# Which copy of an expert's rows the router's dot products read: PSUM or SBUF, chosen by the length of their queue

## The chip, the cores and the metric

The kernel runs on 1 core of one Trainium2 chip. The metric is device time in microseconds (us), from the first to the last instruction of one execution with what lies around it. Five engines each take their own instructions in order: TensorE (PE) multiplies matrices, VectorE (DVE) and ScalarE (ACT) work on rows, GpSimd (POOL) does element-wise work on data in SBUF and issues the gathers and scatters, SyncE (SP) issues the plain loads. They meet only in semaphores.

## The reference

Causal block attention for 4 batches and 8 heads of 576 tokens; its output is a table `x` of 2304 tokens by 512. Two mixture-of-experts layers follow, with 8 experts each and a hidden width of 1024. The second layer picks its expert from the output of the first:

```python
# layer 1, top 2 of 8 experts by noisy logits
h = np.maximum(x[mask] @ w1[e], 0.0)
out[mask] += top2_w[mask, k, None] * (h @ w2[e])
# layer 2, top 1 of 8, logits from the output of layer 1
logits = x @ w_gate + modality_bias[modality_id]
e_idx = np.argmax(logits, axis=1)
h = np.maximum(x[mask] @ w1[e], 0.0)
out[mask] = gate_w[mask, None] * (h @ w2[e])
```

## The kernel before, in words

Attention comes first, then the experts of layer 1, then those of layer 2. The experts run as a list of jobs. A job is one expert and some tiles of 128 tokens: `j00` and `j10` (the first two and three tiles of experts 0 and 1, known early), `j11` (the last two tiles of expert 1), then `firsts`: the last three tiles of expert 0, and five tiles each for experts 2 to 7. `seconds` are the groups of layer 2.

Every fp32 operand is split into a high and a low part (`wh`, `wl` for weights, `xth`, `xtl` for rows, `kp` or `hh`, `hl` for hidden values), and each product is three matmuls. For a job `run` does this:

- `mm1`: for each of 8 hidden slices f, 12 matmuls into a tile `ph` (3 buffers); ACT writes the high part of the hidden values from it, DVE the low part (SCALAR_TENSOR_TENSOR into `kp` or `hl`). `mm2` needs both.
- `mm2`: for each token tile, 24 matmuls into a tile `py` (pool `ps_y`, 3 buffers, `NY`). ACT writes `yr`, the rows of `py` scaled by their gate, to SBUF (5 buffers), POOL scatters `yr` into the table X2. In the gaps between half tiles the next job's rows are transposed (`px`, 1 buffer, filled by PE, read by ACT and DVE) into `xth`, `xtl`.
- The next weights: SP loads `raw`, ACT copies its high part `wh`, and POOL subtracts: `wl` from `raw` and `wh`, both in SBUF (`Stage.split`; in the jobs up to `firsts` always POOL, `[gps]`). Eight such pieces serve a job, four for each of its two layers.

The change touches `note`. For each finished token tile it queues eight dot products, one for each expert of layer 2, which are the logits of layer 2 piece by piece: DVE multiplies a row by a column of `wgb` (in SBUF, broadcast) and accumulates into one column of `yg`. The eighth is followed by a scatter of `yg` into the table LG on POOL. The queue is the list `fill`. `filler` takes from it between the pieces of PE's work, when the planner's clocks say that DVE is not behind. `room` is called before a `py` buffer is taken, and empties the queue until the dots that hold a `py` buffer leave one free.

A dot can read either copy of its row. `direct` says which: `py` in PSUM with the gate as the scalar, or the scaled `yr` in SBUF. Before, it is set as soon as the flag `places` is, some time after `wgb` has been asked for. So the first three tiles of all (`n` = 0, 1, 2) read `yr`, every later one `py`.

The order of PE, ACT and DVE is the order in which this code is run (a manual schedule), with estimated costs that do not depend on which copy a dot reads.

Of the kernel before, what the change touches and what calls it, by code (L numbers as in the profile page):

```python
# [30 lines left out]
def moe_kernel(tc, q, k, v, w_gate, w_noise, noise, w1, w2, mod_id, w_gate2, mod_bias, m2w1, m2w2, out):  # L31
# [72 lines left out]
    with ExitStack() as top:  # L104
# [271 lines left out]
        flags = set()  # L376
# [164 lines left out]
        fill = []  # L541
# [15 lines left out]
        places = {}  # L557
        yg_n = [0]

        def note(yr, py, g, ids, prev, then):  # L560

            n = yg_n[0]
            yg_n[0] += 1
            direct = "places" in flags

            def dot(e):
                yg = places["yg"][n % len(places["yg"])]
                vec.scalar_tensor_tensor(zero, py if direct else yr, g if direct else 1.0, wgb()[:, e], op0=OP.mult, op1=OP.mult,
                                               accum_out=yg[:, e:e + 1])
                if e == E - 1:  # L570
                    place(yg)

            def place(yg):
                i = gps.indirect_dma_start(out=LG, out_offset=bass.IndirectOffsetOnAxis(ap=ids, axis=0),
                                                 in_=yg, in_offset=None, compute_op=OP.add)
                for o in prev:
                    tc.declare_no_dep(i.ins, o.ins, reason="rows of other tokens")
                prev.append(i)
                if then:
                    then()  # L580

            t = clk["pe"] + 1
            fill.extend([(t, lambda e=e: dot(e), direct) for e in range(E)])
# [6 lines left out]
        def add_rows(ids, c0, nt, then=None):  # L590
            last = c0 + nt == NA1
            prev = last_rows if last else []
            placed_ = []

            def f(t, yr, py, g):
                c = c0 + t
                i = gps.indirect_dma_start(out=X2, out_offset=bass.IndirectOffsetOnAxis(ap=ids[:, c:c + 1], axis=0),
                                                 in_=yr, in_offset=None, compute_op=OP.add)
                for o in prev + (early_rows if last else []):
                    tc.declare_no_dep(i.ins, o.ins, reason="rows of other tokens")  # L600
                prev.append(i)
                note(yr, py, g, ids[:, c:c + 1], placed_, then if t == nt - 1 else None)
            return f
# [1069 lines left out]
```

## Time and profile before

| | |
|---|---|
| median of 3 runs | 1015.5 us (1011.27 to 1016.81) |
| the profiled execution | 1010.93 us |
| its span, first to last instruction | 1009.1 us |
| PE, DVE, ACT, POOL busy | 95%, 72%, 51%, 49% of the span |
| DVE dots reading `py` | 296 |
| DVE dots reading `yr` | 24 |

The profile is of one execution, which lies 4.6 us below the median. A time in a timeline row is the start from the beginning of the span. "idle before" in square brackets is how long the engine stood before that instruction, and what it waited for. PE is busy nearly everywhere, so the places where it stands still are few and can be looked at one by one. Jobs `j11` and the first of `firsts`, where the change lies, run from 342 to 408 us.

### The profile page before, as it was taken

What the parts mean: (1) busy time and instruction counts of PE and PEld (TensorE: products, weight loads), DVE (VectorE), ACT (ScalarE), POOL (GpSimd) and SP (SyncE); (2) the same over time, 40 slices, a digit from 0 to 9 for tenths busy, and PEclk for the clock granted to TensorE, in tenths of its full rate; (3) what the DMA queues carried; (4) which work ended last, traced back from release to release, by engine and by line L of the source; (5) the groups of instructions that cost most, each with busy time, mean ns of one, the idle gap of its engine ahead of it and who ended that gap; (6) DMA issues with size and microseconds to landing.
All of it is one profiled execution on the core that took longest, in us unless ns stands there. A gap on an engine that the chain in (4) does not pass through costs nothing.

```text
span 1009.1 us, 17454 instructions
## 1 busy us (share of the span) xinstructions
PE 959.0 (95%) x6058; PEld 866.3 (86%) x6058; DVE 728.1 (72%) x1761; ACT 518.4 (51%) x1156; POOL 496.1 (49%) x400
## 2 busy tenths in 40 slices
PE   7999998898998989999999999999999989999995
PEld 6999887787887978989989898998969879999995
DVE  6887779999967778659394866849789876445540
ACT  5999887668653244333333343333325445555551
POOL 6223333242221578968484866837377254333331
PEclk8999999999999999999999999999999999999998
DMA  5566643321065656656373645625266867666620
GB/s 125 112 165 207 192 123 84 84 70 61 27 201 169 175 115 158 158 138 126 92 144 88 148 104 129 123 73 85 82 160 181 283 215 238 224 220 224 204 89 13
DMA packets 158258, 141.59 MB, mean 140 GB/s; under 512 B 76234, under 2 KB 124746, under 8 KB 158035
## 3 DMA queue, kind: packets, MB, share of 16 engines
q1 hardware_dynamic: 140098, 107.18, 36.0%
q0 software_dynamic: 18064, 33.23, 16.4%
q8 instruction: 50, 0.82, 0.3%
q14 instruction: 46, 0.37, 0.1%
HBM read 112.54 MB, written 28.36 MB: 140 GB/s over the span
## 4 chain that ended last, share of the span: by engine, by line
PE 75%; DVE 13%; issue 4%; ACT 3%; DMA 2%; POOL 2%; SPq 1%; POOLq 0%; ACTq 0%; DVEq 0%
PE ph L71 29%; PE py L71 27%; PE pt L71 8%; PE ps L71 6%; PE pa L71 3%; PE px L71 2%; DVE wl L71 2%; DVE nm L71 2%; DVE PTl L71 2%; DMA xr<-X,ids 1%; ACT p L71 1%; DVE kp L71 1%; POOL wl L71 1%; ACT wh L71 1%; DVE sl_ob L71 1%
## 5 line engine op out<-in xcount | busy, mean ns | idle before, releaser
L71 POOL TENSOR_TENSOR wl<-raw,wh 128x1024 fp32r<-128x1024 f32 x80 | 208.3, 2633 | 107.2 <-ACT wh L71 95.3
L71 PE MATMUL ph<-xth,wh 128*128 128x320 f32 (+2 forms) x800 | 241.3, 302 | 2.1 <-DVE kp L71 2.1
L71 PE MATMUL ph<-xth,wl 128*128 128x320 f32 (+2 forms) x800 | 240.1, 300 | 0.0
L71 PE MATMUL ph<-xtl,wh 128*128 128x320 f32 (+2 forms) x800 | 240.0, 300 | 0.0
L71 DVE SCALAR_TENSOR_TENSOR zero<-py,gts,wgb 128x512 f32<-128x512 f32 x296 | 221.5, 748 | 8.2
L71 PE MATMUL py<-wh,kp 128*128 128x512 f32 x496 | 168.1, 399 | 3.9 <-DVE zero L71 3.9
L71 PEld LDWEIGHTS ph<-xth,wh 128*128 128x128 f32 x800 | 151.7, 190 | 3.7 <-DVE kp L71 2.9
L71 PEld LDWEIGHTS ph<-xtl,wh 128*128 128x128 f32 x800 | 151.7, 190 | 0.7
L71 ACT ACTIVATE wh<-raw 128x1024 fp32r<-128x1024 f32 x144 | 150.8, 1053 | 2.3 <-DMA raw<-in_moe_w_dram 2.3
L71 PEld LDWEIGHTS ph<-xth,wl 128*128 128x128 f32 x800 | 151.7, 190 | 0.0
L71 ACT ACTIVATE yr<-py,gts 128x512 f32<-128x512 f32 x60 | 41.3, 689 | 143.1 <-PE py L71 99.0
L71 PEld LDWEIGHTS py<-wh,kp 128*128 128x128 f32 x496 | 93.9, 189 | 22.7 <-DVE zero L71 4.1
L71 DVE TENSOR_TENSOR wl<-raw,wh 128x1024 fp32r<-128x1024 f32 x64 | 79.9, 1256 | 29.6 <-ACT wh L71 29.5
L71 DVE SCALAR_TENSOR_TENSOR hl<-ph,hh 128x320 fp32r<-128x320 f32 (+2 forms) x100 | 46.4, 466 | 75.2 <-ACT hh L71 74.8
L71 PE MATMUL ps<-kh,kp 128*128 128x256 f32 (+5 forms) x320 | 97.1, 346 | 3.0 <-POOL p L817 1.3
L71 PE MATMUL py<-wl,kp 128*128 128x512 f32 x248 | 97.4, 393 | 0.0
L71 POOL DMA_INDIRECT xr<-X,ids x55 | 59.0, 1073 | 75.0 <-PE px L71 45.3
L71 DVE TENSOR_TENSOR xtl<-px,xth 128x512 fp32r<-128x512 f32 x58 | 40.0, 690 | 75.6 <-ACT xth L71 75.4
L71 PE MATMUL py<-wh,hh 128*128 128x512 f32 x232 | 94.0, 405 | 0.0
L71 PE MATMUL py<-wh,hl 128*128 128x512 f32 x232 | 90.9, 392 | 0.0
L71 PE MATMUL py<-wl,hh 128*128 128x512 f32 x232 | 90.4, 390 | 0.0
L71 ACT ACTIVATE hh<-ph 128x320 fp32r<-128x320 f32 (+2 forms) x100 | 41.8, 418 | 94.3 <-PE ph L71 88.9
(249 smaller groups left out, 1841.4 us busy)
## 6 DMA issues: line engine op xcount, KB each, us to landing
raw<-in_moe_w_dram SPq DMA_DIRECT2D x144, 512.0 KB, 4.3
X<-zero SPq DMA_DIRECT2D x13, 512.0 KB, 3.6
kld<-in_k_dram SPq DMA_DIRECT2D x32, 128.0 KB, 3.1
qld<-in_q_dram SPq DMA_DIRECT2D x32, 128.0 KB, 2.9
vld<-in_v_dram SPq DMA_DIRECT2D x32, 128.0 KB, 2.6
X<-x SPq DMA_DIRECT2D x16, 256.0 KB, 2.4
xs<-in_moe_w_dram SPq DMA_DIRECT2D x4, 512.0 KB, 4.1
wgb<-WG2T POOLq DMA_DIRECT2D x1, 2048.0 KB, 8.6
```

The lines of the kernel that those rows point to most:

```text
L71: return f(*a, **kw)
```

## The change

A tile's dots read `py` only if, besides the flag, at most ten dots are queued when the tile is finished. Otherwise they read `yr`.

```diff
@@ note @@
             n = yg_n[0]
             yg_n[0] += 1
-            direct = "places" in flags
+
+            direct = "places" in flags and len(fill) <= 10
```

When tiles 3 to 6 are finished the queue is longer than ten; from tile 7 on it never is. In all 32 dots change their operand, those of the last two tiles of `j10` and of the two of `j11`.

DVE's row from the end of `mm1` of `j11` to the first `kp` of the next job, before (`zero,yg_4509<-...` is a dot, with the number of its `yg` buffer; `xtl` and `kp` are the low parts of rows and of hidden values, both read from PSUM):

```order
L71 SCALAR_TENSOR_TENSOR zero,yg_4509<-py,gts_106,wgb 128x512 x2
L71 TENSOR_TENSOR xtl<-px,xth 128x4x128
L71 SCALAR_TENSOR_TENSOR zero,yg_4509<-py,gts_106,wgb 128x512 x3
L71 TENSOR_TENSOR xtl<-px,xth 128x4x128
L71 SCALAR_TENSOR_TENSOR zero,yg_4509<-py,gts_106,wgb 128x512 x3
L71 SCALAR_TENSOR_TENSOR zero,yg_4506<-py,gts_106,wgb 128x512
L71 TENSOR_TENSOR xtl<-px,xth 128x4x128
L71 SCALAR_TENSOR_TENSOR zero,yg_4506<-py,gts_106,wgb 128x512 x5
L71 SCALAR_TENSOR_TENSOR kp_4888<-ph,kp_4888 128x384
```

These are the dots of tile 3 (`yg_4509`) and the first of tile 4 (`yg_4506`). The same place now:

```order
L71 SCALAR_TENSOR_TENSOR zero,yg_4509<-yr,wgb 128x512 x2
L71 TENSOR_TENSOR xtl<-px,xth 128x4x128
L71 SCALAR_TENSOR_TENSOR zero,yg_4509<-yr,wgb 128x512 x3
L71 TENSOR_TENSOR xtl<-px,xth 128x4x128
L71 SCALAR_TENSOR_TENSOR zero,yg_4509<-yr,wgb 128x512 x3
L71 SCALAR_TENSOR_TENSOR zero,yg_4506<-yr,wgb 128x512
L71 TENSOR_TENSOR xtl<-px,xth 128x4x128
L71 SCALAR_TENSOR_TENSOR zero,yg_4506<-yr,wgb 128x512 x5
L71 SCALAR_TENSOR_TENSOR kp_4888<-ph,kp_4888 128x384
```

Nothing moves in DVE's order: the same dots stand at the same places, between the same `xtl` and `kp`, with another operand. So it goes on to the last dot of tile 6, two dots and one `kp` or `hl` in turn.

PE's row at the start of the second tile of `j11` (tile 6), with what its instructions wait for:

```order
 L71 MATMUL px<-ident,xr 128x128 [waits DMASW4_49,DVE_49]
 L71 MATMUL px<-ident,xr 128x128 x3
-L71 MATMUL py<-wh,kp_4619 128x512 [waits DVE_49]
+L71 MATMUL py<-wh,kp_4619 128x512
 L71 MATMUL py<-wl,kp_4619 128x512
 L71 MATMUL py<-wh,kp_4619 128x512
```

The first matmul of tile 6 waited for DVE, since its `py` buffer was the one that the dots of tile 3 read. That wait is gone.

POOL's row between the second and the third weight piece for the next job:

```order
 L71 TENSOR_TENSOR wl<-raw,wh 128x1024
+L71 DMA xr<-X_60,ids_100 128x512
 L71 DMA LG<-yg_4509,ids_102 2944x9
-L71 DMA xr<-X_60,ids_100 128x512
 L71 TENSOR_TENSOR wl<-raw,wh 128x1024
```

A gather of rows and the scatter of tile 3's dots change places there.

## Rows read from the trace of the kernel before

**Rows 1.** The page's first part: busy time, share of the span, instructions.
```profile
PE 959.0 (95%) x6058; PEld 866.3 (86%) x6058; DVE 728.1 (72%) x1761; ACT 518.4 (51%) x1156; POOL 496.1 (49%) x400
```

**Rows 2.** Waits, 326 to 420 us: waiter, releaser, total us, times, longest.
```profile
PEld py L71 <- DVE zero L71: 4.1, 1, 4.1
...
PE py L71 <- DVE zero L71: 3.9, 1, 3.9
```

**Rows 3.** Stretches: length, busy PE, PEld, DVE, ACT, POOL, granted clock, DMA, GB/s.
```profile
360.47:364.58 4.11, 0.25 (x4) 0.01 (x2) 3.55 (x10) 2.02 (x3) 3.64 (x4) 0.96 0.38 114
364.58:368.88 4.30, 4.30 (x13) 3.38 (x14) 0.74 (x2) 0.00 (x0) 4.13 (x3) 0.64 0.85 198
354.15:356.91 2.76, 2.76 (x15) 2.22 (x14) 2.65 (x10) 0.39 (x1) 0.13 (x1) 1.00 0.00 0
```

**Rows 4.** DVE's dots, by operand: count, ns (min/median/max), first and last start.
```profile
L71 DVE SCALAR_TENSOR_TENSOR zero<-py,gts,wgb x296: 731/751/755, 356.1 to 778.4; 128x512 f32<-128x512 f32 x148
...
L71 DVE SCALAR_TENSOR_TENSOR zero<-yr,wgb x24: 681/692/695, 335.6 to 355.4; 128x512 f32<-128x512 f32 x24
```

**Rows 5.** DVE's timeline, 356 to 393 us: start, us, what, idle before it.
```profile
356.08 0.75 DVE L71 SCALAR_TENSOR_TENSOR zero<-py,gts,wgb 128x512 f32<-128x512 f32 x1
...
358.18 0.69 DVE L71 TENSOR_TENSOR xtl<-px,xth 128x512 fp32r<-128x512 f32 x1 [0.54 <-ACT xth L71]
...
361.57 0.69 DVE L71 TENSOR_TENSOR xtl<-px,xth 128x512 fp32r<-128x512 f32 x1 [0.45 <-ACT xth L71]
...
363.76 0.75 DVE L71 SCALAR_TENSOR_TENSOR zero<-py,gts,wgb 128x512 f32<-128x512 f32 x1
...
370.14 0.69 DVE L71 TENSOR_TENSOR xtl<-px,xth 128x512 fp32r<-128x512 f32 x1 [4.83 <-ACT xth L71]
...
374.91 0.56 DVE L71 SCALAR_TENSOR_TENSOR kp<-ph,kp 128x384 fp32r<-128x384 f32 x1 [0.23 <-ACT kp L71]
...
393.00 0.69 DVE L71 TENSOR_TENSOR xtl<-px,xth 128x512 fp32r<-128x512 f32 x1
```

**Rows 6.** POOL's timeline, 359 to 393 us.
```profile
359.65 2.38 POOL L71 TENSOR_TENSOR wl<-raw,wh 128x1024 fp32r<-128x1024 f32 x1
...
369.75 1.01 POOL L71 DMA_INDIRECT xr<-X,ids  x1 [0.49 <-PE px L71]
371.14 2.41 POOL L71 TENSOR_TENSOR wl<-raw,wh 128x1024 fp32r<-128x1024 f32 x1 [0.38 <-ACT wh L71]
...
387.76 2.98 POOL L71 TENSOR_TENSOR wl<-raw,wh 128x1024 fp32r<-128x1024 f32 x1
392.39 1.02 POOL L71 DMA_INDIRECT xr<-X,ids  x1 [1.65 <-PE px L71]
```

**Rows 7.** Timelines of POOL and of DVE at two places outside the change.
```profile
154.65 1.56 POOL L71 TENSOR_TENSOR vs<-vld,vs 128x640 fp32r<-128x640 f32 x1
155.40 0.90 DVE L71 SCALAR_TENSOR_TENSOR ex<-u,ex 128x80 f32<-128x80 f32 x1
164.49 0.24 DVE L71 SCALAR_TENSOR_TENSOR ln<-oh,ln 128x80 f32<-128x80 f32 x1
730.40 2.62 POOL L71 TENSOR_TENSOR wl<-raw,wh 128x1024 fp32r<-128x1024 f32 x1 [8.94 <-ACT wh L71]
730.68 2.41 DVE L71 TENSOR_TENSOR sl_oa<-lane,sl_a 128x54 bf16<-128x54 f32 x1
739.25 0.20 DVE L71 TENSOR_TENSOR sl_oa<-lane,sl_a 128x54 bf16<-128x54 f32 x1
```

**Rows 8.** The same two timelines, where POOL's next instruction stands ready behind.
```profile
191.84 2.70 DVE L71 TENSOR_TENSOR wl<-xs,wh 128x512 fp32r<-128x512 f32 x2 [1.05 <-ACT wh L71]
...
193.33 0.66 POOL L71 TENSOR_TENSOR ss<-ss 128x1 f32<-128x1 f32 x1
```

**Rows 9.** PE's timeline: second tile half of the first job of `firsts`.
```profile
393.56 0.39 PE L71 MATMUL py<-wl,hh 128*128 128x512 f32 x1
...
394.69 0.60 PE L71 MATMUL px<-ident,xr 128*128 128x128 f32 x4
```

## The prediction

> **What bounds the kernel now.** I read the busy times first: PE works 95% of the span, everything else 72% or less [rows 1]. So a change counts if it takes away a stretch in which PE stands, or makes one. Next I read the waits between 326 and 420 us, the jobs in which dots change their operand: PE waits for a dot there once, for 4 us [rows 2]. The stretches show that place: PE is idle from 360.47 to 364.58, and after it PE needs 4.30 us for the same twelve `py` matmuls that took 2.76 us at 354.15 [rows 3]. The granted clock is 0.64 over those 4.30 us and 1.00 in the earlier stretch: PE came back at the lower of its two levels, 1.2 GHz, and rose to 2.4 GHz on the way. The standstill costs 4.11 + 1.54 = 5.65 us. Then I read the two engines that could take its place, DVE [rows 5] and POOL [rows 6], and last the places where these two work on SBUF at the same time [rows 7, 8], which is what the changed dots will do.
>
> **What the change removes.** The four tiles' dots no longer hold a `py` buffer, so the first matmul of tile 6 waits for nothing but an ACT copy long done. PE could go on 5.65 us earlier from here on.
>
> **What it makes shorter.** A dot takes 751 ns from `py` and 692 ns from `yr` [rows 4]: 32 dots by 0.06 us is 1.9 us of DVE.
>
> **What it adds.** A dot from `py` reads one operand in SBUF (`wgb`), a dot from `yr` reads two (`yr` and `wgb`). The 24 such dots of before all run before 356.1 us [rows 4], where POOL issues only gathers and scatters; the first `wl` of this stretch begins at 359.65 [rows 6]. So no row shows a `yr` dot beside a `wl`, and its price must be taken from the nearest rows. These are plain. At 730.68 a DVE instruction with two operands in SBUF takes 2.41 us, and ends at 733.09; POOL's `wl`, begun at 730.40, ends at 733.02. The same instruction takes 0.20 us at 739.25 with no `wl` beside it. At 155.40 a SCALAR_TENSOR_TENSOR, the operation of the dots, with two SBUF operands takes 0.90 us and ends at 156.30, right after POOL's subtraction (154.65 + 1.56 = 156.21); one of the same size takes 0.24 us at 164.49 [rows 7]. So DVE stands until POOL's instruction is over. The dots from `py` show nothing of it: 731 to 755 ns, all 296 of them, with many of POOL's `wl` beside them [rows 4]. And it goes in turn: at 193.33 a POOL instruction on 128x1 lasts 0.66 us while one of two waiting DVE subtractions goes first, and the pair of them ends at 194.54 [rows 8]. So between two `wl` that follow each other, one dot gets through and the second stands again.
>
> The Trainium skill has this as a rule ("SBUF — State Buffer", section "Who interferes with whom"): a VectorE instruction with two SBUF inputs contends with a GpSimd instruction that reads SBUF, whoever starts first holds the shared ports for its whole instruction, and the other fully blocks. The rows agree (733.09 behind 733.02). Taken at its word for all eight `wl` below, with a dot always ready, it gives 8 by 2.4 = 19.2 us of standing in place of my 17.7, that is 1026.3 us, inside my range.
>
> **The price.** From 359.65 to 390.74 (387.76 + 2.98) POOL computes eight `wl`, the second half of the weights of the next job among them. One takes 2.4 us (2.38, 2.41; the 2.98 of the last begins while the issue before it still runs) [rows 6]. In that stretch DVE's queue is 32 dots with 11 instructions between them that read PSUM (`xtl`, `kp`, `hl`). Up to the first `kp` dots stand in a row of two to six, so a `wl` meets a dot at once: the full 2.4 us. In `mm1` two dots and one `kp` or `hl` alternate; a `wl` that meets the latter lets it pass (0.5 us) and costs 1.9 us. I count five full and three with a `kp` or `hl` first: 5 by 2.4 + 3 by 1.9 = 17.7 us. Bounds: below, only the five (12.0 us); above, all eight full (19.2 us). I take 17.7, since in both row pairs of [rows 7] the instruction stood for the whole rest of POOL's.
>
> **The sum goes by DVE's queue,** which is then last. Behind the standing dots, in order, are the `xtl` (rows of the next job), and the `kp` and `hl` without which `ph` does not come free and `mm2` cannot go on; PE waits for these, and with PE the evictions and weight copies of ACT. Before, DVE goes from 356.08 to the `xtl` at 393.00 [rows 5]: 36.9 us, of which it is idle 0.54 + 0.45 + 4.83 + 0.23 = 6.05 us, so 30.9 us of work. The 4.83 us are the standstill itself: DVE waited for PE, which had waited for DVE. After: 30.9 − 1.9 + 17.7 = 46.7 us of work and standing, with 0.5 us of idle left at the first `xtl`. That `xtl` then starts at 356.08 + 47.2 = 403.3 and ends at 404.0. `px` has one buffer, so the transposes that PE does at 394.69 before [rows 9] wait for it: 9.3 us later. The 5.65 us that PE gains are inside this, and so is a slow restart of its clock, as long as DVE is last. The bounds: 12.0 us of standing gives +3.6 us, 19.2 us gives +10.8 us; two slow restarts by 1.54 us that DVE does not hide would make that +13.9 us.
>
> After this tile DVE reads `py` again and stands for no `wl`; all that follows is timed from PE, which is busy to the end. The shift stays. The profiled execution would be 1010.93 + 9.3 = 1020.2 us. It lies 4.6 us below the median of the runs, so the median would be 1015.5 + 9.3 = **1024.8 us**, 0.9% slower. What a measurement of this kernel can tell from no change is about 0.5%, 5.1 us.
>
> The gather and the scatter that change places on POOL cost nothing by themselves: the gather waited 0.49 us for PE's `px` [rows 6], and what the scatter feeds is read only after the last expert. No DMA is added.
>
> **Rivals.**
>
> *No collision (faster or the same).* If the dots from `yr` do not stand beside `wl`, PE starts tile 6 at 360.47. For it: the 24 dots on record took 692 ns throughout. Against it: nothing that reads SBUF ran on POOL beside them, and both row pairs of [rows 7]. Its time: the 5.65 us are not all kept, since POOL becomes last. It works without a gap up to the last `wl`, 390.74, and only the 0.49 and 0.38 us at 369.75 and 371.14 can shrink, by about 0.5 us in all. The matmul that reads this `wl`, at 393.56 before [rows 9], could go at 387.9 and would wait to 390.2: 3.3 us are kept, 1012.2 us. Without POOL's limit 1009.9 us. Chance 9%: about half of it beyond the 0.5%.
>
> *Collision, but hidden.* DVE's 4.83 us of idle and the 5.65 us of PE take it in, if only every other `wl` meets a dot: 4 by 2.4 = 9.6 us of standing gives +1.2 us, 1016.7 us. The point where it turns is 8.4 us of standing; three and a half `wl` do it. Against it: dots are most of DVE's queue, and all eight `wl` lie in it. Chance 6%, no change.
>
> *Worse than forecast.* DVE stays last and PE, standing for several us at a time, comes back at the lower clock again and again, on top of all eight `wl` at their full length: the +13.9 us above, 1029.4 us. Chance 15%.
>
> That the change does not do what it says is no case: in the order of DVE exactly 32 dots have the other operand, and the wait of PE is gone.
>
> **How the numbers follow.** Forecast 70%, worse 15%, hidden 6%, no collision 9%. Slower by over 0.5%: 70 + 15, less 3 for the lower bound of +3.6 us = 82%. Faster by over 0.5%: 5%. The rest, 13%, within. The range has to hold the forecast, from 1015.5 + 3.6 = 1019.1, and most of the worse case; the three runs lie between 1011.27 and 1016.81, and a median could as well come out some 3 us lower, so it begins at 1016 and ends at 1031.
>
> **What would show it.** Right: of the dots from `yr`, now 56, some eight of the 32 take 2 to 3 us, each ending where a `wl` of POOL ends, and their mean rises from 0.69 to about 1.0 us; PE no longer waits for a dot at tile 6, but for `kp`, `hl` and `xtl` of DVE between 363 and 405 us, some 10 to 15 us in all; the transposes of 394.69 stand near 404; from there every start is later by one constant. Wrong: all dots from `yr` at 0.69 us beside `wl`, or the standing there and the transposes no later than before. If the `wl` too take 3 us, the order in which the two engines take turns is other than I read it.

## The result, and the profile after

The changed kernel takes 1024.35 us (median of 6 runs, 1023.08 to 1028.19), the kernel before 1013.46 us (6 runs, 1010.98 to 1016.81): a ratio of 1.0114, 95% interval 1.0094 to 1.0133, that is 9.5 to 13.5 us slower. The profiled execution takes 1024.1 us, its span is 1022.2 us. Up to 358 us this trace runs 0.41 us later than that of before (the `xtl` of 358.18 in [rows 5] stands at 358.59); that is taken off where positions are compared.

The page's first part, against [rows 1]: PE gains nothing, DVE is busy 18.7 us longer.

```profile
PE 963.1 (94%) x6058; PEld 868.9 (85%) x6058; DVE 746.8 (73%) x1761; ACT 519.0 (51%) x1156; POOL 495.3 (48%) x400
```

The dots by operand, against [rows 4]. The median from `yr` is still 692 ns; the longest is 5952.

```profile
L71 DVE SCALAR_TENSOR_TENSOR zero<-py,gts,wgb x264: 735/751/754, 409.4 to 790.9; 128x512 f32<-128x512 f32 x132
...
L71 DVE SCALAR_TENSOR_TENSOR zero<-yr,wgb x56: 674/692/5952, 335.2 to 406.1; 128x512 f32<-128x512 f32 x56
```

DVE's timeline shows which ones. Here are all dots over 0.8 us (each other one takes 0.67 to 0.69), and the `xtl` that stood at 393.00 before.

```profile
359.92 3.10 DVE L71 SCALAR_TENSOR_TENSOR zero<-yr,wgb 128x512 f32<-128x512 f32 x1
...
365.01 3.77 DVE L71 SCALAR_TENSOR_TENSOR zero<-yr,wgb 128x512 f32<-128x512 f32 x1
...
370.78 4.06 DVE L71 SCALAR_TENSOR_TENSOR zero<-yr,wgb 128x512 f32<-128x512 f32 x1
...
375.62 5.95 DVE L71 SCALAR_TENSOR_TENSOR zero<-yr,wgb 128x512 f32<-128x512 f32 x1
...
385.97 3.70 DVE L71 SCALAR_TENSOR_TENSOR zero<-yr,wgb 128x512 f32<-128x512 f32 x1
...
390.07 2.41 DVE L71 SCALAR_TENSOR_TENSOR zero<-yr,wgb 128x512 f32<-128x512 f32 x1
...
397.96 3.72 DVE L71 SCALAR_TENSOR_TENSOR zero<-yr,wgb 128x512 f32<-128x512 f32 x1
...
406.70 0.69 DVE L71 TENSOR_TENSOR xtl<-px,xth 128x512 fp32r<-128x512 f32 x1
```

Seven dots take 26.71 us; less 7 by 0.69 that is 21.9 us of standing. Each of them ends 0.55 or 0.56 us behind the end of a `wl`. In POOL's timeline, the counterpart of [rows 6]:

```profile
360.05 2.41 POOL L71 TENSOR_TENSOR wl<-raw,wh 128x1024 fp32r<-128x1024 f32 x1
...
365.25 2.97 POOL L71 TENSOR_TENSOR wl<-raw,wh 128x1024 fp32r<-128x1024 f32 x1
...
371.36 2.93 POOL L71 TENSOR_TENSOR wl<-raw,wh 128x1024 fp32r<-128x1024 f32 x1
...
375.76 5.25 POOL L71 TENSOR_TENSOR wl<-raw,wh 128x1024 fp32r<-128x1024 f32 x2
385.14 1.56 POOL L71 DMA_INDIRECT LG<-yg,ids  x1 [4.13 <-DVE zero L71]
386.15 2.97 POOL L71 TENSOR_TENSOR wl<-raw,wh 128x1024 fp32r<-128x1024 f32 x1
389.33 2.60 POOL L71 TENSOR_TENSOR wl<-raw,wh 128x1024 fp32r<-128x1024 f32 x1 [0.22 <-ACT wh L71]
...
398.15 2.97 POOL L71 TENSOR_TENSOR wl<-raw,wh 128x1024 fp32r<-128x1024 f32 x1
```

The `wl` of 365.25 ends at 368.22 and the dot of 365.01 at 368.78. The two `wl` of 375.76 end at 381.01 and one dot, that of 375.62, at 381.57: it stood for both. This standing lies inside the recorded lengths of the dots, and the profile gives no semaphore for it: DVE and POOL meet in more than the semaphores named at the start. POOL then waits for DVE in its turn, since the scatter `LG` needs the late dots (4.13 us). PE's waits from 326 to 420 us, against [rows 2]:

```profile
PE ph L71 <- DVE kp L71: 5.9, 2, 4.7
PE px L71 <- DVE xtl L71: 3.5, 2, 2.9
PE ph L71 <- DVE xtl L71: 2.9, 1, 2.9
```

The wait for a dot at tile 6 is gone. In its place PE waits 12.3 us for `kp` and `xtl`. Two stretches (length, then busy PE, PEld, DVE, ACT, POOL, granted clock, DMA, GB/s) show PE coming back below its upper level of 2.4 GHz, by turns as in [rows 3]; in the second one it is at the lower level, 1.2 GHz, throughout:

```profile
371.00:374.00 3.00, 3.00 (x12) 3.00 (x13) 3.00 (x1) 0.00 (x0) 3.00 (x2) 0.64 0.54 160
...
383.57:386.50 2.93, 2.93 (x9) 2.93 (x10) 2.86 (x8) 0.00 (x0) 1.36 (x2) 0.50 0.12 42
```

The transposes of 394.69 in [rows 9] come here:

```profile
407.44 0.66 PE L71 MATMUL px<-ident,xr 128*128 128x128 f32 x4 [2.91 <-DVE xtl L71]
```

That is 12.3 us later, the 0.41 taken off, and from there to the end every start keeps that distance within 0.7 us.

### The profile page after: what moved, and what is told of

It is laid out like the page before. It is cut to its first block, busy times and chain, and to the rows that moved or that the text cites. A ratio compares the mean times of both kernels' runs of the same rounds, so it can differ in the third digit from the quotient of the medians.

```text
span 1022.2 us, 17455 instructions
## 1 busy us (share of the span) xinstructions
PE 963.1 (94%) x6058; PEld 868.9 (85%) x6058; DVE 746.8 (73%) x1761; ACT 519.0 (51%) x1156; POOL 495.3 (48%) x400
## 4 chain that ended last, share of the span: by engine, by line
PE 70%; DVE 17%; issue 4%; ACT 4%; POOL 2%; DMA 2%; SPq 1%; POOLq 0%; ACTq 0%
PE ph L71 27%; PE py L71 25%; PE pt L71 7%; PE ps L71 5%; DVE zero L71 4%; PE pa L71 3%; PE px L71 2%; DVE wl L71 2%; DVE nm L71 2%; DVE PTl L71 2%; ACT p L71 1%; DMA xr<-X,ids 1%; DVE kp L71 1%; POOL wl L71 1%; ACT wh L71 1%
## 5 line engine op out<-in xcount | busy, mean ns | idle before, releaser
L71 DVE SCALAR_TENSOR_TENSOR zero<-py,gts,wgb 128x512 f32<-128x512 f32 x264 | 197.6, 749 | 7.4
L71 PEld LDWEIGHTS ph<-xtl,wh 128*128 128x128 f32 x800 | 153.8, 192 | 4.0 <-DVE xtl L71 3.3
```

The costliest lines, as they stand in the source:

```text
L71: return f(*a, **kw)
```

## The experiments

Each ratio is against runs of the kernel before on the same chip. The theory is that of the prediction: a dot with two operands in SBUF stands while POOL's `wl` runs, and DVE's queue hands that on. The first four kernels test it part by part.

**One operand in SBUF (e1_one_sbuf).** The kernel after, with

```diff
+                if not direct and "places" in flags and n > 2:
+                    vec.tensor_scalar(zero, yr, 1.0, 0.0, op0=OP.mult, op1=OP.add, accum_out=yg[:, e:e + 1])
+                else:
+                    vec.scalar_tensor_tensor(...
```

> The kernel after, but the 32 changed dots are replaced by a tensor_scalar with accumulator that reads yr as its only operand in SBUF. It leaves out the product with wgb for them, so the logits of layer 2 of tiles 3 to 6 are other numbers and the groups of layer 2 may come out in other sizes: beside the time, the start of the px transposes that stand at 394.69 before and 407.44 after is compared. Theory (the second operand in SBUF makes the dots stand while wl runs): each of the 32 takes at most 0.75 us, none of 2 us or more; PE's wait at tile 6 is gone and DVE stands nowhere; px near 391, that is 3.3 us earlier than before (bounds 0 and 5.65). Rival (the delay comes from reading the row later out of yr, its buffers, or the exchanged gather and scatter on POOL, whatever the number of operands): px stays near 407, 11 to 13 us later than before.

1008.69 us against 1012.07, ratio 0.9962 (0.9947 to 0.9976): 3.4 us faster, not 11 slower. None of the 32 stands, beside the same `wl`:

```profile
L71 DVE TENSOR_SCALAR_CACHE_REDUCE zero<-yr x32: 674/686/689, 357.4 to 387.8; 128x512 f32<-128x512 f32 x32
```

So it is the second operand in SBUF, and neither `yr` nor the exchange on POOL. DVE's `kp` at 375 to 387 us come 5.6 us earlier than before, which is the whole 5.65 us of the prediction's first step. Then most of it goes:

```profile
391.56 0.50 PE L71 MATMUL py<-wl,hh 128*128 128x512 f32 x1 [2.14 <-POOL wl L71]
```

That is the limit the "no collision" rival named: POOL's last `wl`. It let this matmul go on at 390.2 and put what is kept at 3.3 us; here it starts at 390.3, once the 1.3 us are taken off by which this trace ran late before the change. The transposes of 397.90 of before are only 1.6 us earlier (397.61), while the median is 3.4 us lower; the profiled execution, 1011.02 us, is the slowest of the four. Since these dots leave out the product, the groups of layer 2 may differ, so the times up to 398 us say more here than the median does.

**Only tile 3 (e2_tile3).** The kernel before, with

```diff
-            direct = "places" in flags
+            direct = "places" in flags and n != 3
```

> The kernel before with only the eight dots of tile 3 reading yr. PE's wait at tile 6 goes (worth 5.65 us at most); these dots run beside two of the wl. Theory (standing per wl, prices as measured after: 3.1 + 3.8 us less 0.7 each): two long dots of 2.4 to 3.8 us, DVE's gain and loss nearly cancel, px of 394.69 within -2 to +2 us, time between 3 us faster and 1 us slower than before. Rival A (the delay does not grow with the number of wl met, one meeting is enough to tip DVE's queue): +9 us or more. Rival B (no standing, the wait alone counts): -5.65 us.

1012.16 against 1012.07 us, ratio 0.9997 (0.9986 to 1.0007). Two dots stand:

```profile
361.18 3.12 DVE L71 SCALAR_TENSOR_TENSOR zero<-yr,wgb 128x512 f32<-128x512 f32 x1
...
366.30 3.77 DVE L71 SCALAR_TENSOR_TENSOR zero<-yr,wgb 128x512 f32<-128x512 f32 x1
```

5.5 us of standing, less 8 by 0.06 for the shorter dots, is 5.0 us, against the 5.65 that PE gains at tile 6. PE gives them back right behind these dots: it waits 0.57 us and then 2.96 us for `xtl`, and comes back at a granted clock of 0.56, which costs another 1.6 us (0.44 by 3.74). The second wait, and the stretch behind it:

```profile
372.26 0.44 PE L71 MATMUL ph<-xtl,wh 128*128 128x384 f32 x1 [2.96 <-DVE xtl L71]
```

```profile
372.26:376.00 3.74, 3.73 (x13) 3.74 (x14) 3.60 (x10) 0.17 (x1) 3.57 (x3) 0.56 0.41 90
```

The two cancel, and the transposes of 394.69 are where they were, at 396.38 in a trace that runs 1.7 us late from before the change on. So the cost grows with the number of `wl` met, and the wait removed does have a worth.

**Only tiles 5 and 6 (e3_tiles56).** The same line with `n not in (5, 6)`.

> The kernel before with only the 16 dots of tiles 5 and 6 reading yr. PE's wait of 4.11 us at tile 6 stays. These dots run in the mm1 of the next job, from about 376 us on, beside the last four wl. Theory: three or four long dots, each ending where a wl ends, 2.4 to 3.7 us, about 8 to 11 us of standing less 1 us by shorter dots: px of 394.69 comes 7 to 11 us later, and the time is 7 to 11 us longer than before. Were the two wl that run one behind the other to meet no dot this time, +5. Rival (the time lost after comes from tile 6's earlier start and what follows it, not from these dots): 0.

1018.93 us, ratio 1.0071 (1.0052 to 1.0090): 6.9 us slower, just below the 7 to 11 us expected, and for another reason than I had given. The standing is larger than I said:

```profile
377.33 5.66 DVE L71 SCALAR_TENSOR_TENSOR zero<-yr,wgb 128x512 f32<-128x512 f32 x1
...
384.12 5.57 DVE L71 SCALAR_TENSOR_TENSOR zero<-yr,wgb 128x512 f32<-128x512 f32 x1
...
393.36 3.69 DVE L71 SCALAR_TENSOR_TENSOR zero<-yr,wgb 128x512 f32<-128x512 f32 x1
```

12.9 us by these three, twice for two `wl` in a row. But PE's wait at tile 6, which I expected to stay, is not there:

```profile
363.70 0.50 PE L71 MATMUL py<-wh,kp 128*128 128x512 f32 x1 [0.39 <-ACT yr L71]
```

Tile 5's buffer is free as soon as ACT has copied it, and tile 6 took that one. So this kernel has a gain too: with the 4.9 us that e4_last3 shows below, 12.9 less 1.0 less 4.9 is 7.0 us. That is the median's 6.9, but the trace itself has only 5.5 us at the transposes of 394.69 (402.81, in a trace that ran 2.6 us late before the change); where the other 1.5 us of the sum went is open.

**Only the last three dots of tile 3 (e4_last3).** The kernel before, with

```diff
+            reads_py = [places_set and not (n == 3 and e > 4) for e in range(E)]
...
+                d = reads_py[e]
+                vec.scalar_tensor_tensor(zero, py if d else yr, g if d else 1.0, wgb()[:, e], ...
```

> The kernel before with only the last three dots of tile 3 (e = 5, 6, 7) reading yr. The py buffer comes free with the dot e = 4, and PE may start tile 6 at 361.2 instead of 364.58. These three dots come to run between about 361.7 and 364.5, between the end of one wl (362.03 before) and the start of the next (364.55 before). Theory (a dot from yr costs nothing where no wl runs): at most one of the three stands, for under 0.6 us; PE's wait at tile 6 shrinks from 4.1 to under 1 us, its clock stays at the higher level, and the kernel is 3.3 us faster than before (2.5 to 5). Rival A (any dot from yr in this stretch costs a standing of 2.4 us or more): 0 to +2. Rival B (POOL's wl or DVE's xtl of the next job give the gain back): 0, with PE waiting 3 us later on for one of them.

1011.65 us, ratio 0.9995 (0.9983 to 1.0007): no gain, though the first half of the theory holds (no dot from `yr` over 0.694 us, PE waits 0.5 us at tile 6 and goes on at full clock, and DVE's `kp` at 370 to 387 us are 4.9 us earlier). Rival B is what happened:

```profile
390.98 0.50 PE L71 MATMUL py<-wl,hh 128*128 128x512 f32 x1 [1.99 <-POOL wl L71]
```

```profile
388.00:392.00 4.00, 2.01 (x9) 1.33 (x8) 0.94 (x3) 0.94 (x1) 3.84 (x3) 1.00 0.48 131
392.00:396.00 4.00, 4.00 (x14) 3.23 (x13) 1.90 (x4) 2.23 (x3) 3.69 (x3) 0.57 0.64 196
```

PE stands for 2 us behind POOL's last `wl` and then works at a clock of 0.57: 2.0 + 0.43 by 4 = 3.7 us, and with that 3.9 of the 4.9 us are given back by the transposes of 404.30 (here 403.43, in a trace that ran 0.1 us late). A stall of 2 us here costs nearly twice its length.

**POOL's queue cleared (e5_late_lg).** e4_last3 and, on POOL, the two scatters `LG` of tiles 4 and 5 behind that `wl`:

```diff
-                    place(yg)
+                    late.append(lambda: place(yg))
+                    hold = {4: 1, 5: 2, 6: 2, 7: 1}.get(n, 0)
+                    while len(late) > hold:
+                        with tc.issue_after(last_b[0]) if 6 <= n <= 8 else ExitStack():
+                            late.pop(0)()
```

> The kernel of e4_last3, and on POOL the two LG scatters of tiles 4 and 5 (1.05 us of its time each) issued after the last wl of the second-half weights instead of ahead of it; nothing else changes its place. In e4_last3 PE came 4.9 us earlier up to 387 us, then waited 2.0 us for that wl and ran the next 4 us at a clock of 0.57, which left 0.9 us. Theory (POOL's queue is what gave the gain back): that wl ends 2.1 us earlier, at about 388.8, PE does not wait for it or for under 0.3 us, its clock stays at the higher level, and 4 to 5 us are kept at the px transposes that stand at 403 to 404: about 1007.5 us beside a kernel before of 1012.1, 0.4 to 0.5% faster. Rival (the weights' loads or ACT's high parts are no earlier): the five wl in a row stop for ACT wh, PE waits as before, and the time is that of e4_last3.

1007.19 us against 1011.95, ratio 0.9948 (0.9931 to 0.9965): 4.8 us faster than before, and by the two ratios 1.6% below the changed kernel. POOL now does the five `wl` in a row, the last one ends at 387.28, and PE stands no more (timeline, then a stretch):

```profile
374.89 12.39 POOL L71 TENSOR_TENSOR wl<-raw,wh 128x1024 fp32r<-128x1024 f32 x5
```

```profile
388.00:392.00 4.00, 4.00 (x21) 3.32 (x20) 1.58 (x5) 2.80 (x4) 1.00 (x1) 1.00 0.59 154
```

**The scatters alone (e8_lg_only).** The kernel before with only the edit on POOL.

> The kernel before with only the two LG scatters of tiles 4 and 5 behind the last wl of the second-half weights, as in e5_late_lg; every dot keeps its operand of before. Theory: PE still waits for a dot at tile 6 (4.1 us) and does not wait for that wl, so nothing is gained: 0, within 1 us. Rival (POOL's queue bounds this stretch by itself): 1 to 2 us faster.

1013.46 us, ratio 1.0007 (0.9988 to 1.0026): no change. The two limits lie one behind the other, and taking away either alone brings nothing that can be measured (e4_last3, e8_lg_only), both together 4.8 us.

**Every dot from `yr` (e7_all_yr).** `direct = False`.

> The kernel before with every dot of all tiles reading yr, 296 changed dots in place of 32. It asks whether the standing is general, and whether a DVE with time to spare hides it. Theory: in the steady jobs (58 us each, eight wl, DVE idle for about 17.8 us of the 58) each wl meets a dot, some 2.7 us of standing each, 21.9 us a job less 2.4 us by shorter dots: 19.5 us against 17.8 us of idle, so DVE is nearly full. With all of its idle usable the five steady jobs would add 5 times 1.7 us to what the first stretch costs, about 1032 us; with little of it usable, 5 times 8 us, about 1062 us. I take 1045. Long dots: about 50 to 60 of 320, and no dot from py. Rival (only the crowded first stretch stands): within 3 us of the kernel after, 1021 to 1027 us, with some eight long dots in all.

1109.47 us (two runs), ratio 1.0953 (1.0925 to 1.0982). The rival falls, and so does my number of 1045, by 64 us. One steady job (a second dot of 3.65 us, at 491.01, is not among the rows):

```profile
472.94 3.05 DVE L71 SCALAR_TENSOR_TENSOR zero<-yr,wgb 128x512 f32<-128x512 f32 x1
...
483.58 3.65 DVE L71 SCALAR_TENSOR_TENSOR zero<-yr,wgb 128x512 f32<-128x512 f32 x1
...
503.38 6.06 DVE L71 SCALAR_TENSOR_TENSOR zero<-yr,wgb 128x512 f32<-128x512 f32 x1
...
522.22 0.49 DVE L71 SCALAR_TENSOR_TENSOR hl<-ph,hh 128x320 fp32r<-128x320 f32 x1 [1.27 <-ACT hh L71]
```

```profile
472.94:544.23 71.29, 63.36 (x333) 57.42 (x332) 51.30 (x102) 20.79 (x34) 42.42 (x24) 0.90 0.40 96
```

A job takes 71.29 us where it took 58. Only four dots stand, for five of the eight `wl` (34 long dots in all, not 50 to 60), 13.7 us of standing. Nearly all of it shows, 13.3 us (the next three jobs take 69.9 to 70.1 us): PE is idle for 7.9 us and its 58 us of work take 63.4 at a clock of 0.90. DVE's idle time hides none of it, because it lies elsewhere: the dots come early in the job, in front of the `kp` that PE waits for, and DVE idles later, where no dot is left (1.27 us ahead of each `hl`). Over the whole kernel the 34 long dots stand 110.9 us; less 296 by 0.06 for the shorter dots that is 93.1 us, and the kernel is 97.5 us longer.

**Who goes first.** The prediction read [rows 8] as taking turns, and the 5.95 us dot speaks against it. e6_halves splits each `wl` of the kernel after in two (`k = 512`).

> The kernel after, with each wl of this stretch computed by two POOL subtractions of 128x512 in place of one of 128x1024. It tells who goes first when POOL's next subtraction stands ready behind the one that a dot waits for. Theory A (POOL's next ready one goes ahead of the waiting dot, as the 5.95 us of one dot beside two wl suggest): the long dots are as long as after, 2.4 to 6 us, seven or so of them, no more than one for a whole wl; time that of after, up to 2 us more. Theory B (they take turns): dots of 1.2 to 2 us, one for each half, 12 to 16 of them, none over 2.5 us; POOL's wl are spread out by the dots between, and the time is within 3 us of after.

1027.57 us, ratio 1.0146 (1.0121 to 1.0172). Both happen in one kernel:

```profile
376.76 6.23 DVE L71 SCALAR_TENSOR_TENSOR zero<-yr,wgb 128x512 f32<-128x512 f32 x1
...
391.62 1.29 DVE L71 SCALAR_TENSOR_TENSOR zero<-yr,wgb 128x512 f32<-128x512 f32 x1
...
392.95 1.66 DVE L71 SCALAR_TENSOR_TENSOR zero<-yr,wgb 128x512 f32<-128x512 f32 x1
```

The first stood for four halves in a row (376.91 to 382.43), the other two for one each. So neither theory holds alone. Three small programs measured it apart from the kernel.

> Not the kernel: a program that computes none of the outputs and only lets DVE and POOL run beside each other on tiles of the kernel's shapes, in parts that both engines begin together. It measures the disputed cost by itself, and who goes first. Part 1: dots from yr alone, 8. Part 2: wl alone, 4. Part 3: 6 wl in a row beside 12 dots from yr. Part 4: 6 wl beside 16 dots from py. Part 5: 6 wl beside 16 tensor_scalar with accumulator that read yr alone. Part 6: gather and wl in turn, 4 each, beside 16 dots from yr. Part 7: 4 gathers beside 10 dots from yr. Part 8: 12 wl halves (128x512) beside 16 dots from yr. Part 9: 8 memsets of 128x1024 on POOL beside 12 dots from yr. Theory A (POOL's next ready one goes first): in part 3 one dot stands for all six wl, 14 us or more, and the others take 0.69; in part 8 the same. Theory B (they take turns): in part 3 six dots of about 3.1 us (2.4 and 0.7), each wl recorded about 0.6 us longer; in part 8 twelve of about 1.9 us. Both: parts 4, 5, 7 at 0.67 to 0.75 us throughout; in part 6 four dots of about 3 us, more if the issue of a gather stands with them; part 9 open, 0.69 us if only POOL's reads count.

Part 3: turns. Six `wl` take 16.07 us, and six dots that follow each other 2.86 or 2.70 us each, among them:

```profile
21.69 2.70 DVE L59 SCALAR_TENSOR_TENSOR zero<-yr,wgb 128x512 f32<-128x512 f32 x1
```

Part 8: twelve dots of 1.62 to 1.77 us. Parts 4 and 5, beside six `wl`: 0.69 us throughout, from `py` or with `yr` alone. Part 7, beside gathers: 0.69. Part 9, beside memsets, which only write: 0.69. Part 6: 2.98 to 3.17 us, one dot for each `wl`.

> A second program like p1_ports that computes none of the outputs. In p1_ports dots and wl took turns, yet in the kernel after one dot stood for two wl (5.95 us). It asks whether an issue of a gather or a scatter on POOL just ahead makes the difference. Part 1: 4 wl in a row, dots from yr beside them. Part 2: a gather, then 4 wl; the dots begin during the gather's issue. Part 3: the same, but three dots from py come first, so that the first dot from yr begins inside the first wl. Part 4: a gather, then 8 halves. Part 5: gather and two wl, three times. Part 6: gather, two wl, gather, four wl. Part 7: a scatter, then 4 wl. Theory D (a dot that begins during the issue stands for the whole row of wl behind it): one dot of about 10 us in part 2, of about 5.5 us three times in part 5, 10 us in parts 4 and 7; turns of 2.7 us in parts 1 and 3. Theory B (turns always): no dot over 3.3 us in any part.

Turns in every part, 2.70 us (1.62 with halves), and 3.67 for the first dot behind a scatter: theory D fell here. But beside it ran the kernel after with the two scatters moved:

> The kernel after, with the two LG scatters of tiles 4 and 5 behind the last wl as in e5_late_lg, so that five wl follow each other on POOL behind one scatter of rows. Theory D (a dot that begins during a DMA issue stands for the whole row of wl behind it): one dot of 8 to 13 us in place of 5.95, 3.70 and 2.41, and the time is that of after or up to 3 us longer. Theory B (turns): the 5.95 us dot becomes several of 2.7 us, one for each wl, none over 4 us; time 1 to 3 us less than after.

1024.54 us, ratio 1.0112 (1.0085 to 1.0139), as after. Not five but three `wl` follow each other, since POOL then waits 8.32 us for the next high part from ACT; one dot stood for all three (DVE, then POOL):

```profile
378.08 8.25 DVE L71 SCALAR_TENSOR_TENSOR zero<-yr,wgb 128x512 f32<-128x512 f32 x1
```

```profile
378.23 7.54 POOL L71 TENSOR_TENSOR wl<-raw,wh 128x1024 fp32r<-128x1024 f32 x3
```

The programs differed from the kernel in that all their `wl` wrote one tile, and so each waited for the one before it. The last one gave them tiles of their own.

> A third program that computes none of the outputs. In p2_after_gather every wl wrote the same tile, so that each waited for the one before it to be over, and dots and wl took turns; in the kernel each wl has tiles of its own, and in e9_after_late one dot stood for three of them (8.25 us). Here the wl have four sets of tiles. Part 1: 4 wl into four tiles beside 12 dots from yr. Part 2: a gather first. Part 3: a scatter first. Part 4: a scatter, then 4 wl into one tile, as in p2_after_gather. Part 5: as part 3, but four dots from py first, so that the first dot from yr begins inside a wl. Part 6: a scatter, 4 wl that read one pair of tiles and write four. Part 7: as part 3, with the high parts written by ACT just ahead. Part 8: a scatter, two wl, a scatter, four wl; DVE has two dots from yr and one from py in turn. Theory E (a wl that need not wait for the one before it follows without a gap, and the dot waits on): one dot of about 10 us (4 wl) in parts 2, 3, 6 and perhaps 1, turns of 2.7 us in part 4; if it also holds for a dot that begins inside a wl, 8 to 9 us in part 5. Theory F (something else in the kernel): turns of 2.7 us in all parts.

Theory E, with one reserve. Part 3 and part 4, a scatter and four `wl`, into four tiles and into one (DVE, then POOL):

```profile
44.66 10.52 DVE L62 SCALAR_TENSOR_TENSOR zero<-yr,wgb 128x512 f32<-128x512 f32 x1
...
63.29 3.61 DVE L62 SCALAR_TENSOR_TENSOR zero<-yr,wgb 128x512 f32<-128x512 f32 x1
66.94 2.70 DVE L62 SCALAR_TENSOR_TENSOR zero<-yr,wgb 128x512 f32<-128x512 f32 x1
```

```profile
44.83 9.79 POOL L85 TENSOR_TENSOR wl<-raw,wh 128x1024 fp32r<-128x1024 f32 x4
...
63.44 11.15 POOL L81 TENSOR_TENSOR wl<-raw,wh 128x1024 fp32r<-128x1024 f32 x4
```

One dot of 10.08, 10.52, 10.49 and 10.48 us in parts 2, 3, 6 and 7; 8.78 in part 5, where it began inside a `wl`; 5.90 and 9.71 in part 8 for two and four. Turns in part 4. The reserve is part 1: four tiles, but no gather or scatter ahead, and turns there too (2.85, 2.70). So a dot stands for a whole row where both are given: the `wl` do not wait for each other, and the row begins behind a gather or a scatter. e6_halves fits: its row at 376.91 begins behind a scatter, and the half before 391.62 began at 390.75, when ACT had just written the high part (389.62 + 1.05 us). Why the DMA issue ahead matters was not found.

## Why the prediction was right, and where not

- **The wait removed.** 5.65 us, as priced: e1 has 5.6 us and e4 4.9 us of it (its wait shrinks to 0.5 us), at DVE's `kp` behind the place.
- **Shorter dots.** As priced, 0.06 us each.
- **The collision.** Shown: two operands in SBUF stand beside `wl` (e2, e3, e7, p1), one does not (e1, p1).
- **The size of the standing is the step that failed.** "Five full and three with a `kp` or `hl` first: 5 by 2.4 + 3 by 1.9 = 17.7 us." Measured 21.9. The count of eight `wl` was right. But only one was met late (1.72 us, at 390.07), not three; and a `wl` behind a scatter holds DVE for some 3 us, not 2.4: the dots of 365.01, 370.78, 385.97 and 397.96 stood 3.0 to 3.4 us each, and the first dots behind a scatter in p2 and p3 (3.67 and 3.61 us) stood 2.9 to 3.0 us. The rows had shown it: the 2.98 in [rows 6] I had put down to a start recorded too early and taken 2.4. It was not the only one. Four of the eight `wl` of before begin behind a scatter, and these are the rows that [rows 6] leaves out:

```profile
364.55 2.95 POOL L71 TENSOR_TENSOR wl<-raw,wh 128x1024 fp32r<-128x1024 f32 x1
...
374.74 5.33 POOL L71 TENSOR_TENSOR wl<-raw,wh 128x1024 fp32r<-128x1024 f32 x2
...
381.26 5.32 POOL L71 TENSOR_TENSOR wl<-raw,wh 128x1024 fp32r<-128x1024 f32 x2
```

With them the eight lengths, as recorded, add up to 21.4 us, close to the 21.9 measured. My upper bound of 19.2 us fell short as well. So did the time by the Trainium skill's rule ("SBUF — State Buffer", "Who interferes with whom"), which I had also worked out with 8 by 2.4.
- **"And it goes in turn [...]. So between two `wl` that follow each other, one dot gets through and the second stands again."** Wrong for the two `wl` of 375.76, where one dot stood for both. It changed nothing in the sum, since DVE stands as long as POOL works either way: e9, with a row of three, takes the time of after. The 2.70 us of p1 are 2.0 + 0.69, the rest of a `wl` and the dot. The Trainium skill ("SBUF — State Buffer", "SBUF: two separate sides") says that whichever of the two starts first holds the shared ports for its whole instruction. The turns of p1 agree with it; the 10.52 us of p3 go beyond it. Nor can one tell from the recorded starts who was first: six of the seven long dots begin 0.13 to 0.58 us ahead of the `wl` for which they stood (370.78 ahead of 371.36).
- **DVE's queue as the sum.** Right in kind: from the first long dot to the `xtl` of 406.70 DVE has no idle time of its own. With 21.9 for 17.7 the sum puts that `xtl` at 407.9 in this trace, 1.2 us too late. About 1.0 of them are small waits of before that I had counted as work: two dots and a `kp` take 2.08 us there (from 376.99 to 379.07), after 1.81 (from 382.97 to 384.78), and only 0.12 of the 0.27 are the shorter dots; that is 0.15 for each of seven. PE's slow restarts were inside, as argued: the stretches at 0.64 and 0.50 cost PE some 2.5 us (0.36 by 3.00 + 0.50 by 2.93), and nothing is added to DVE's sum. So the rival "worse" had its size from the wrong term.
- **The time.** 1024.8 forecast, 1024.35 measured, and the nearness is partly luck: the shift is 12.3 us at the transposes and 10.9 between the medians, where I had 9.3, and I had added it to a median of three runs (1015.5) that lies 2.0 us above that of six, and 3.4 above that of the 23 runs that stand beside e1 to e4 (1012.07). Against those 23 the change would cost 12.3 us, as at the transposes: a shift too small by 3 us met a start too high by 3.
- **No collision.** Ruled out for this kernel, and its limit by POOL's last `wl` confirmed in e1 and e4. **Hidden.** Ruled out for this kernel. My turning point of 8.4 us of standing, three and a half `wl`, was neither confirmed nor refuted: after, 9.6 of the 21.9 us were taken in (21.9 less 12.3), in e3 7.4 of 12.9, and in e2 all 5.5, two `wl`, which yet left nothing of what PE had gained. So no single amount of standing marks the turn.

## What to carry to other kernels

An element-wise instruction of DVE with two operands in SBUF cost, in this kernel, the rest of whatever POOL was subtracting beside it; before moving an operand from PSUM to SBUF to free a bank, look for POOL's rows in that stretch and add their recorded lengths, as they stand, to DVE's queue (here 21.4 us, with 21.9 measured). Move only the instructions that hold the bank (here three dots, in a gap of POOL), and then look at which engine comes last next: the gain of 4.9 us was kept only when POOL's queue was shortened too. Idle time that DVE has later does not make up for standing in front of an instruction for which PE waits (e2, e7).

## What the runs showed of the hardware beyond what was expected

- DVE waiting for POOL is not always one instruction long. A row of POOL subtractions that do not wait for each other, behind a gather or a scatter, held one dot for 10.1 to 10.5 us (four) or 5.9 us (two); where each waits for the one before, dot and `wl` alternate at 2.70 us.
- The first dot beside a row of `wl` stands longer than the next ones: 3.61 and 3.67 us behind a scatter, 2.98 to 3.20 behind a gather, against 2.70 in turns. A part of this is only where the dot begins: in part 4 of p3 the first begins 0.15 us ahead of its `wl` (63.29 and 63.44), the second 0.52 us inside the next (66.94 and 66.42). Another part is that a `wl` right behind a scatter is recorded at 2.9 to 3.0 us, and at 2.3 to 2.4 behind a gather.
- The issue of a gather alone does not hold a dot (0.69 us in part 7 of p1), nor does that of a scatter: in the trace of before five dots from `yr` begin during the scatters from 341.87 to 350.88 us, and each takes 0.68 or 0.69 us.
- POOL's memset beside dots from `yr` costs nothing (0.69 us, part 9 of p1). The Trainium skill ("SBUF — State Buffer", "Who interferes with whom") says that a GpSimd instruction that only writes does not contend with two SBUF inputs; this agrees.
- PE's idle time of 2.0 us in e4_last3 was followed by 4 us at a granted clock of 0.57, and cost 3.7 us in all.
